# Block 0 of a fused attention, SwiGLU and top-2 kernel in one explicit order of single steps

## The chip, the cores and the metric

The kernel runs on one core of a Trainium2 chip. The metric is the device time of one execution in microseconds; before the change it is 1103.71 us, the median of three runs (1103.06 to 1104.98).

## What is computed

Three layers in a row, all in float32 at the outside:

```
attn = softmax(window 64, causal)(q k^T / 8) v          # 4 batches, 8 heads, 576 rows, 64 wide
x    = attn as 2304 rows of 512
xn   = x / sqrt(mean(x*x) + 1e-6) * rms_g
x2   = (silu(xn @ w_gate) * (xn @ w_val)) @ w_out         # d_ff 1536; these three weights arrive as float64
out  = top-2 of 8 experts over x2, relu MLP 512 -> 1024 -> 512 each, gate-weighted sum
```

The order of the parts matters here: the 2304 rows go through attention and SwiGLU in six blocks, and the float64 weights are turned into pairs of float32r words while the first of them is worked on.

## The kernel before

**Blocks and steps.** A block is 384 rows. Its attention comes in 8 groups (n = 8j to 8j+7, a group is 192 rows of two heads). A group has `att_s` (scores, PE), `att_m` (mask and row minimum on DVE, exponential on ACT, 1/sum on DVE, the product `pm` on POOL), `att_p` (transpose on PE, copy on ACT) and `att_v` (PE, copy into `xT` on ACT). When a block's `xT` is there, `norm_a`, `norm_b`, `norm_c` make the RMS norm and split the result into a high and a low float32r part, `xnH` and `xnL`. Then 12 steps s = 12j + fc follow, one for each 128 columns of d_ff: `m1_half(s, 0)` and `m1_half(s, 1)` are 12 matmuls each (gate and value; three products of high and low parts for each of four k-tiles), `m1_tanh` and `m1_h` make the activation `hh`, and `m1_out` adds 9 matmuls into the block's output.

**Weights.** A chunk fc of a weight is one page of 4 KB a partition, 512 float64 numbers as pairs of 32-bit words; column c is 0 for gate, 1 for value, 2 for out. `load_w` brings it from SP's queue. `conv_a` (L320, L321) scales both words in place on ACT, `conv_b` clamps the high words in place (L332; on POOL for c in `CLP` and fc > 1, otherwise on DVE) and assembles float32 with two bit operations on DVE (L334, L335) into the pages `gv` and `wo`. All these operands but the last output stand two words apart. `split_w` makes the float32r pair for a step: high part on ACT (`gvH` L343, `woHL` L354), low part by a subtraction (`gvL` L346: gate half on DVE, value half on POOL for s in `GH`; `woHL` L355 on POOL). All 36 chunks are converted during block 0; `gv` and `wo` stay for the other five blocks. In blocks 1 to 5 a step has only the splits.

**Who sets the order.** Up to the last part the instructions are placed by a scheduler: the code fills numbered slots (`at`, `run`), and the scheduler may still move an instruction past others on its engine. Each engine then executes its own list strictly in that order. Of the conversions ahead of step 0, chunk 0 of gate and value comes in slot 16; the rest of chunks 0 and 1 is held behind the norm of block 0 (`after_norm`, tied to L300 and L302 of chosen k-tiles). The last part of the kernel (experts) is under `tc.manual_schedule()`, where the order written is the order issued.

**Norm of block 0.** `norm_a(0)` lets PE multiply `xT` by itself (12 matmuls of 128x128, L262) and takes the diagonals with DVE (L266). The other blocks square on ACT, add on POOL (L273, L274) and sum with a column of ones.

Of the kernel before, what the change touches and what calls it, by code (L numbers as in the profile page):

```python
# [24 lines left out]
def tile_window_attention_swiglu_top2(  # L25
# [107 lines left out]
    WL = (5, 5, 7, 13, 17)  # L133
    CS = (16, 16, 16, 16, 16)
    CLP = (0, 2)
    GH = range(1, 12)
    HLP = range(0, 12, 2)
# [5 lines left out]
    NKT, NPM, NPT = 5, 3, 2  # L143
# [46 lines left out]
    Pm, PT = {}, {}  # L190
# [17 lines left out]
    def att_m(n):  # L208
        first = (n // HP) % GS == 0
        ps = SC.pop(n)  # L210
        p = attn.tile([P, 3, P], F32, name=f"pm{n}", tag="pm", bufs=NPM)
        st = attn.tile([P, 3, 4], F32, name=f"st{n}", tag="st", bufs=NPM)
        for i in range(3):
            m = mask0 if first and i == 0 else mask
            nc.vector.tensor_tensor_reduce(out=p[:, i, :], in0=ps[:, i, :], in1=m, scale=-0.125, scalar=MASKED,
                                           op0=ALU.add, op1=ALU.min, accum_out=st[:, i, 0:1])
        for i in range(3):
            nc.scalar.activation(p[:, i, :], p[:, i, :], AF.Exp, bias=st[:, i, 0:1], scale=-1.0,
                                 accum_out=st[:, i, 1:2])
        nc.vector.tensor_scalar(st[:, :, 2], st[:, :, 1], 1e-9, None, op0=ALU.add)  # L220
        nc.vector.reciprocal(st[:, :, 3], st[:, :, 2])  # L221
        nc.gpsimd.tensor_tensor(p, p, st[:, :, 3:4].to_broadcast([P, 3, P]), op=ALU.mult)  # L222
        Pm[n] = p

    def att_p(n):
        p = Pm.pop(n)
        ps = bank(f"pp{n}", [P, 3, P])
        for i in range(3):
            nc.tensor.transpose(ps[:, i, :], p[:, i, :], ident)
        t = attn.tile([P, 3, P], F32, name=f"pT{n}", tag="pT", bufs=NPT)  # L230
# [3 lines left out]
    def att_v(n):  # L234
# [3 lines left out]
        if n < 2 * HP:  # L238
            ps = psum.tile([P, 3, 64], F32, name=f"pv{n}", tag=f"x2_{n % 3}", bufs=1)
        else:  # L240
            ps = bank(f"pv{n}", [P, 3, 64])
        for i in range(3):
            for h in range(2):
                s, o = slice(64 * h, 64 * h + 64), 64 * (h ^ (n & 1))
                nc.tensor.matmul(ps[s, i, :], w[:, i, 2 * (n % 2) + h, :], t[:, i, o:o + 64], start=True, stop=True)
        rb, hp = divmod(n, HP)
# [7 lines left out]

    def norm_a(j):
        x = xT[j]
        if j == 0:
            ps = bank(f"ss{j}", [P, TT, P])
            for t in range(TT):
                c = slice(t * P, t * P + P)  # L260
                for kk in range(KD):
                    nc.tensor.matmul(ps[:, t, :], x[:, kk, c], x[:, kk, c], start=kk == 0, stop=kk == KD - 1)  # L262
            SQ[j] = work.tile([P, TT], F32, name="ssd")
            for t in range(TT):
                sq = work.tile([P, KD, P], F32, name=f"sq{j}_{t}", tag="sq", bufs=2)
# [12 lines left out]
    def norm_b(j):
        ps = SQ.pop(j)
        r = work.tile([P, 2, TT], F32, name=f"rs{j}", tag="rs", bufs=2)  # L280
        nc.vector.tensor_scalar(r[:, 0], ps[:, :TT], 1.0 / DM, 1e-6, op0=ALU.mult, op1=ALU.add)
        nc.gpsimd.tensor_tensor(r[:, 1], r[:, 0], half, op=ALU.pow)
        SS[j] = r

    NI = {}

    def after_norm(f, *a):
        with tc.issue_after(NI[0, PK[0]][0]), tc.issue_after(NI[0, PK[1]][1]):
            f(*a)

    def norm_c(j):
        r = SS.pop(j)
        x = xT.pop(j)
        ps = bank(f"rb{j}", [P, TT, P])
        for t in range(TT):
            nc.tensor.transpose(ps[:, t, :], r[:, 1, t:t + 1].to_broadcast([P, P]), ident)
        xnH[j] = work.tile([P, KD, TB], F32R, name=f"xnH{j}", tag="xnH", bufs=2)
        xnL[j] = work.tile([P, KD, TB], F32R, name=f"xnL{j}", tag="xnL", bufs=2)
        for kk in range(KD):
            v = nc.vector.scalar_tensor_tensor(x[:, kk, :], x[:, kk, :], grow[:, kk:kk + 1],  # L300
                                               ps.rearrange("p t c -> p (t c)"), op0=ALU.mult, op1=ALU.mult)
            a = nc.scalar.activation(xnH[j][:, kk, :], x[:, kk, :], AF.Copy)  # L302
            NI[j, kk] = (v.ins, a.ins)
            nc.vector.tensor_tensor(xnL[j][:, kk, :], x[:, kk, :], xnH[j][:, kk, :].bitcast(F32), op=ALU.subtract)  # L304
# [829 lines left out]
```

## Time and profile before

| | us |
|---|---|
| median of 3 runs | 1103.71 |
| the profiled execution | 1102.57 |
| its span, first to last instruction | 1100.8 |
| TensorE busy | 1039.7 |
| VectorE busy | 612.3 |
| ScalarE busy | 521.7 |
| GpSimd busy | 436.1 |

The mean granted TensorE clock was 0.981 of full speed. PE stands for TensorE's matmuls, DVE for VectorE, ACT for ScalarE, POOL for GpSimd, SP for the engine whose queue issues the loads. Busy times are over the whole span; the change is in its first sixth, so the windows and groups further down are of that stretch. A busy DVE or POOL instruction may be one that waits inside for something that the record doesn't name: its duration then exceeds that of the same instruction elsewhere.

### The profile page before, as it was taken

To read this page: it belongs to the slowest core of one execution; us is meant where nothing else is said; L and a number is where in the kernel's file an instruction comes from. 1 tells how busy PE (TensorE), PEld (TensorE's weight loads), DVE (VectorE), ACT (ScalarE), POOL (GpSimd) and SP (SyncE) were. 2 spreads that over 40 slices of the span, in tenths; PEclk is the share of its full clock that TensorE was granted. 3 is DMA by queue.
4 is the path that set the end of the run, shared out by engine and by line. 5 is a ranking of instruction groups with operands and counts; after the bars stand their busy time and mean duration, and the time that the engine had idled before them with its cause. 6 is when DMAs were issued, how large, how long until landed. Compare 5 with 4: busy or idle time off the path is not lost. (4 is left out here: it accounts for less than half of the span.)

```text
span 1100.8 us, 17727 instructions
## 1 busy us (share of the span) xinstructions
PE 1039.7 (94%) x6548; PEld 912.4 (83%) x6548; DVE 612.3 (56%) x1590; ACT 521.7 (47%) x1169; POOL 436.1 (40%) x450
## 2 busy tenths in 40 slices
PE   5688889999999999999999999999999999999993
PEld 4576778898889889888989888888989898988882
DVE  5799986656566575656666742533424343434420
ACT  6767755555555555555553513433434343433420
POOL 3377653352254226225422336344343444444311
PEclk9699989999999999999999999999999999999997
DMA  8745416121110211100020406444454445545312
GB/s 252 246 140 186 156 53 241 54 59 37 30 34 27 69 31 37 36 1 1 1 77 27 137 13 195 109 134 92 128 104 142 96 142 102 145 96 157 73 16 27
DMA packets 55224, 101.91 MB, mean 93 GB/s; under 512 B 11136, under 2 KB 30320, under 8 KB 55136
## 3 DMA queue, kind: packets, MB, share of 16 engines
q0 software_dynamic: 17904, 49.07, 18.3%
q1 hardware_dynamic: 37232, 51.68, 14.6%
q8 instruction: 53, 0.87, 0.3%
q14 instruction: 35, 0.29, 0.1%
HBM read 80.81 MB, written 19.92 MB: 92 GB/s over the span
## 5 line engine op out<-in xcount | busy, mean ns | idle before, releaser
L369 PE MATMUL gv<-xnH,gvH 128*128 128x384 f32 x576 | 203.4, 356 | 8.3 <-ACT gvH L343 6.0
L864 PE MATMUL y<-wH,hh 128*128 128x512 f32 (+1 forms) x608 | 202.3, 399 | 0.3 <-issue 0.3
L369 PE MATMUL gv<-xnH,gvL 128*128 128x384 f32 x576 | 196.3, 343 | 3.6 <-DVE gvL L346 3.6
L369 PE MATMUL gv<-xnL,gvH 128*128 128x384 f32 x576 | 196.6, 344 | 2.4 <-DVE xnL L304 2.4
L402 PE MATMUL x<-woHL,hh 128*128 128x512 f32 x648 | 174.3, 405 | 6.9 <-ACT hh L387 4.3
L355 POOL TENSOR_TENSOR woHL<-wo,woHL 128x512 fp32r<-128x512 f32 x72 | 99.0, 1380 | 148.4 <-ACT woHL L354 147.9
L402 PEld LDWEIGHTS x<-woHL,hh 128*128 128x128 f32 x648 | 118.9, 190 | 31.8 <-ACT hh L387 5.1
L864 PEld LDWEIGHTS y<-wH,hh 128*128 128x128 f32 (+1 forms) x608 | 112.8, 186 | 29.3 <-issue 0.3
L886 POOL DMA_INDIRECT out_dram<-ys,tid x38 | 63.0, 1658 | 184.8 <-ACT ys L879 136.0
L571 DVE TENSOR_TENSOR wL<-st,wH 128x1024 fp32r<-128x1024 f32 x64 | 78.3, 1226 | 99.6 <-ACT wH L570 96.4
L684 PE MATMUL h<-xph,wL 128*128 128x272 f32 (+3 forms) x448 | 133.4, 298 | 0.1
L684 PE MATMUL h<-xpl,wH 128*128 128x272 f32 (+3 forms) x448 | 133.4, 298 | 0.0
L684 PE MATMUL h<-xph,wH 128*128 128x272 f32 (+3 forms) x448 | 133.3, 298 | 0.0
L694 DVE SCALAR_TENSOR_TENSOR hh<-h,hh 128x272 fp32r<-128x272 f32 (+6 forms) x232 | 69.8, 326 | 105.8 <-ACT hh L690 86.8
L864 PE MATMUL y<-wL,hh 128*128 128x512 f32 (+2 forms) x328 | 128.4, 395 | 0.0
L690 ACT ACTIVATE hh<-h 128x160 fp32r<-128x160 f32 (+4 forms) x184 | 61.7, 344 | 133.0 <-PE h L684 95.1
L369 PEld LDWEIGHTS gv<-xnH,gvH 128*128 128x128 f32 x576 | 109.5, 191 | 15.9 <-ACT gvH L343 7.1
L369 PEld LDWEIGHTS gv<-xnH,gvL 128*128 128x128 f32 x576 | 109.6, 190 | 6.3 <-DVE gvL L346 5.6
L369 PEld LDWEIGHTS gv<-xnL,gvH 128*128 128x128 f32 x576 | 109.8, 191 | 5.2 <-DVE xnL L304 2.9
L346 DVE TENSOR_TENSOR gvL<-gv,gvH 128x1024 fp32r<-128x1024 f32 (+1 forms) x73 | 92.0, 1261 | 25.3 <-ACT gvH L343 15.3
L343 ACT ACTIVATE gvH<-gv 128x1024 fp32r<-128x1024 f32 x72 | 75.8, 1052 | 30.5 <-DVE gv L335 13.8
L222 POOL TENSOR_TENSOR pm<-pm,st 128x384 f32<-128x384 f32 x48 | 41.6, 868 | 119.2 <-DVE st L221 67.7
(198 smaller groups left out, 1803.2 us busy)
## 6 DMA issues: line engine op xcount, KB each, us to landing
vw<-in_v_dram SPq DMA_DIRECT2D x64, 128.0 KB, 2.6
raw<-in_moe_w_gate_dram SPq DMA_DIRECT2D x12, 512.0 KB, 4.4
raw<-in_moe_w_val_dram SPq DMA_DIRECT2D x12, 512.0 KB, 5.7
raw<-in_moe_w_out_dram SPq DMA_DIRECT2D x12, 512.0 KB, 5.7
out_dram<-zero SPq DMA_DIRECT2D x1, 4864.0 KB
qT<-in_q_dram SPq DMA_DIRECT2D x48, 96.0 KB, 2.4
x2d<-xs SPq DMA_DIRECT2D x18, 256.0 KB, 2.3
st<-in_moe_w_dram SPq DMA_DIRECT2D x8, 512.0 KB, 3.6
```

Source lines behind the costliest of these rows:

```text
L222: nc.gpsimd.tensor_tensor(p, p, st[:, :, 3:4].to_broadcast([P, 3, P]), op=ALU.mult)
L343: nc.scalar.activation(h, gv[fc], AF.Copy)
L346: eng.tensor_tensor(l[:, f], gv[fc][:, f], h[:, f].bitcast(F32), op=ALU.subtract)
L355: nc.gpsimd.tensor_tensor(o[:, 512:], wo[fc], o[:, :512].bitcast(F32), op=ALU.subtract)
L369: nc.tensor.matmul(ps, a, b, start=n == 0, stop=n == 3 * KD - 1)
L402: nc.tensor.matmul(X2[j][t], a, b, start=fc == 0 and n == 0, stop=fc == NF - 1 and n == 2)
L571: nc.vector.tensor_tensor(lo, a, ho.bitcast(F32), op=ALU.subtract)
L684: nc.tensor.matmul(ps, w, x, start=i == 0, stop=i == 3 * KD - 1)
L690: nc.scalar.activation(hh[:, c0 - p0:c1 - p0], ps[:, c0 - lo:c1 - lo], AF.Relu)
L694: nc.vector.scalar_tensor_tensor(hh[:, l.start + a - s.start:l.start + b - s.start], ps[:, a + p0 - lo:b + p0 - lo], 0.0, hh[:, a:b].bitca ...
L864: nc.tensor.matmul(ps[:a.shape[1]], a, b, start=i == 0, stop=i == len(terms) - 1)
L886: nc.gpsimd.indirect_dma_start(out=out, out_offset=bass.IndirectOffsetOnAxis(ap=r[:m], axis=0), in_=y[:m], in_offset=None, compute_op=ALU. ...
```

## The change

`att_m`, `att_p`, `att_v`, the norm, the conversion, the split and the activation are cut into single steps, each of one instruction or one row of equal ones. A table `ORDER` names all steps from the first load to the activation of step 11, with the splits of step 12, and is played under `tc.manual_schedule()`. From step 12 on the old slots go on. Besides that:

- `conv_hi` writes the scaled high words straight into `gv` or `wo`, and `conv_lo` writes the low words into the first half of the raw page, so the clamp, the shift and the last bit operation have operands without gaps.
- `CLP` has all three columns: for fc > 1 the value column's clamp is on POOL too (10 more there).
- `GH` starts at 0: the value half of `gvL` of step 0 is on POOL. `HLP`, the steps whose low part of `hh` is on POOL, is 0, 1, 2, 7, 10, 11 in place of the even ones.
- The squares for block 0's norm are made on POOL per group (`first_sq`, 8 products and 4 sums of 128x192) and summed by PE with a column of ones (`first_sum`).
- Pages of chunk 3 and later are loaded only after the second matmul row of step fc - 3 (`DONE`); `late_loads` waits for that of step 11. The attention probabilities `pm` have 4 buffers in place of 3.

```diff
-    CLP = (0, 2)
-    GH = range(1, 12)
-    HLP = range(0, 12, 2)
+    CLP = (0, 1, 2)
+    GH = (0, 1, 2, 3, 4, 5, 6, 7, 8, 9, 10, 11)
+    HLP = (0, 1, 2, 7, 10, 11)
-    NKT, NPM, NPT = 5, 3, 2
+    NKT, NPM, NPT = 5, 4, 2
...
-            ps = psum.tile([P, 3, 64], F32, name=f"pv{n}", tag=f"x2_{n % 3}", bufs=1)
+            ps = psum.tile([P, 3, 64], F32, name=f"pv{n}", tag=f"x2_{n % 2}", bufs=1)
...
+    def first_sq(n):
+        rb, hp = divmod(n, HP)
+        if hp == 0:
+            SS[-1 - rb] = work.tile([P, KD, P], F32, name=f"sq0_{rb}", tag="sq", bufs=2).rearrange("p k c -> p (k c)")
+        sq, one = SS[-1 - rb][:, 0:RG], SS[-1 - rb][:, RG:2 * RG]
+        x = xT[0][:, hp, rb * RG:rb * RG + RG]
+        nc.gpsimd.tensor_tensor(one if hp else sq, x, x, op=ALU.mult)
+        if 0 < hp < HP - 1:
+            nc.gpsimd.tensor_tensor(sq, sq, one, op=ALU.add)
...
-        hi, lo = raw[:, :, 1].bitcast(F32), raw[:, :, 0]
-        nc.scalar.activation(hi, hi, AF.Copy, scale=2.0 ** -112)
-        nc.scalar.activation(lo, lo.bitcast(U32), AF.Copy, scale=0.936 * 2.0 ** -29)
+    def conv_hi(fc, c):
+        words = RAW[fc, c].rearrange("p (n w) -> p n w", w=2)
+        nc.scalar.activation(target(fc, c), words[:, :, 1].bitcast(F32), AF.Copy, scale=2.0 ** -112)
+
+    def conv_lo(fc, c):
+        raw = RAW[fc, c]
+        words = raw.rearrange("p (n w) -> p n w", w=2)
+        nc.scalar.activation(raw[:, :512], words[:, :, 0].bitcast(U32), AF.Copy, scale=0.936 * 2.0 ** -29)
+
+    def conv_clamp(fc, c):
+        hi = target(fc, c)
+        (nc.gpsimd if c in CLP and fc > 1 else nc.vector).tensor_scalar(hi, hi, F64_HI, -F64_HI, op0=ALU.min, op1=ALU.max)
+
+    def conv_shift(fc, c):
+        hi, lo = target(fc, c).bitcast(I32), RAW[fc, c][:, :512]
         nc.vector.scalar_tensor_tensor(lo, hi, 3, lo, op0=ALU.logical_shift_left, op1=ALU.bitwise_or)
+    def conv_sign(fc, c):
+        hi, lo = target(fc, c).bitcast(I32), RAW.pop((fc, c))[:, :512]
+        nc.vector.scalar_tensor_tensor(hi, hi, -0x80000000, lo, op0=ALU.bitwise_and, op1=ALU.bitwise_or)
...
-    at(16, after_norm, conv_a, 0, 2)
-    at(16, after_norm, conv_b, 0, 2)
-    at(16, after_norm, split_o, 0)
-    for c in range(3):
-        at(17, after_norm, conv_a, 1, c)
-        at(17, after_norm, conv_b, 1, c)
...
+    def load_page(fc, c):
+        if fc < WL:
+            return load_w(fc, (c,))
+        with tc.issue_after(DONE[fc - WL]):
+            load_w(fc, (c,))
...
+    ORDER = """
+        L0 L1 L2 S0 L3 L4 M0 M1 E0 S2 E1 N0 U0 L5 N1 T0 M2 U1 M3 E2 L6 T1 E3 N2 U2 S4 C0 N3 C1 U3 w L7 V0 M4 M5
...
+    """
+    in_order = ExitStack()
+    in_order.enter_context(tc.manual_schedule())
+    for op in ORDER.split():
+        KIND[op[0]](*map(int, op[1:].split(".") if op[1:] else ()))
...
+    def after_first():
+        with tc.issue_after(DONE[NF - 1]):
+            late_loads()
...
-    for s in range(NB * NF):
+    for s in range(NF, NB * NF):
```

How it moves instructions shows at three places. The first is ACT's list around the split of block 0's normed rows (`xnH`). In the kernel before it reads:

```order
L249 ACTIVATE xT_273<-pv_431 128x192
L302 ACTIVATE xnH_472<-xT_273 128x384
L320 ACTIVATE raw_2_325<-raw_2_325 128x512
L321 ACTIVATE raw_2_325<-raw_2_325 128x512
L320 ACTIVATE raw_0_439<-raw_0_439 128x512
L321 ACTIVATE raw_0_439<-raw_0_439 128x512
L320 ACTIVATE raw_1_441<-raw_1_441 128x512
L321 ACTIVATE raw_1_441<-raw_1_441 128x512
L320 ACTIVATE raw_2_443<-raw_2_443 128x512
L321 ACTIVATE raw_2_443<-raw_2_443 128x512
L302 ACTIVATE xnH_472<-xT_273 128x384 x3
```

In the changed kernel, from the last copy of block 0's attention (L267) on, where L335 is the `xnH` copy, L370 `conv_hi`, L375 `conv_lo` and L393 `gvH`:

```order
L267 ACTIVATE xT_305<-pv_502 128x192
L375 ACTIVATE raw_1_339<-raw_1_339 128x512
L370 ACTIVATE wo_538<-raw_2_366 128x512
L375 ACTIVATE raw_2_366<-raw_2_366 128x512
L222 ACTIVATE pm_496,st_497<-pm_496,st_497 128x128 x3
L393 ACTIVATE gvH_563<-gv_420 128x1024
L370 ACTIVATE wo_538<-raw_2_536 128x512
L335 ACTIVATE xnH_561<-xT_305 128x384 x3
L370 ACTIVATE gv_585<-raw_0_547 128x512
L335 ACTIVATE xnH_561<-xT_305 128x384
```

Four chunks' conversions stood between the first and the second `xnH`; now one instruction stands between the third and the fourth, and most of chunk 1's conversion lies ahead of the first.

The second place is DVE's list at the same point. Before, from the multiplication by the norm (L300) on:

```order
L300 SCALAR_TENSOR_TENSOR xT_273<-xT_273,grow,rb_468 128x384 x4
L304 TENSOR_TENSOR xnL_473<-xT_273,xnH_472 128x384
L332 TENSOR_SCALAR raw_2_325<-raw_2_325 128x512
L332 TENSOR_SCALAR raw_0_439<-raw_0_439 128x512
L334 SCALAR_TENSOR_TENSOR raw_2_325<-raw_2_325 128x512
L334 SCALAR_TENSOR_TENSOR raw_0_439<-raw_0_439 128x512
L332 TENSOR_SCALAR raw_1_441<-raw_1_441 128x512
L335 SCALAR_TENSOR_TENSOR wo_504<-raw_2_325 128x512
```

And now (L331 is that multiplication, L338 `xnL`, L398 `gvL`, L383 and L387 the two bit operations):

```order
L331 SCALAR_TENSOR_TENSOR xT_305<-xT_305,grow,rb_557 128x384 x3
L338 TENSOR_TENSOR xnL_562<-xT_305,xnH_561 128x384
L331 SCALAR_TENSOR_TENSOR xT_305<-xT_305,grow,rb_557 128x384
L338 TENSOR_TENSOR xnL_562<-xT_305,xnH_561 128x384 x3
L398 TENSOR_TENSOR gvL_564<-gv_420,gvH_563 128x512
L383 SCALAR_TENSOR_TENSOR raw_2_366<-wo_538,raw_2_366 128x512
L387 SCALAR_TENSOR_TENSOR wo_538<-wo_538,raw_2_366 128x512
```

The four `xnL` stand together, and the low part of step 1's gate half comes right behind them.

The third place is POOL's list in the middle of block 0. Before, around the splits of steps 4 and 5:

```order
L332 TENSOR_SCALAR raw_0_787<-raw_0_787 128x512
L346 TENSOR_TENSOR gvL_896<-gv_781,gvH_895 128x512
L355 TENSOR_TENSOR woHL_900<-wo_859,woHL_900 128x512
L332 TENSOR_SCALAR raw_2_791<-raw_2_791 128x512
L346 TENSOR_TENSOR gvL_998<-gv_903,gvH_997 128x512
L332 TENSOR_SCALAR raw_0_909<-raw_0_909 128x512
L355 TENSOR_TENSOR woHL_1002<-wo_859,woHL_1002 128x512
```

And now, around the same splits (L379 is the clamp, L398 `gvL`, L406 the low part of `woHL`):

```order
L398 TENSOR_TENSOR gvL_1100<-gv_886,gvH_1099 128x512
L379 TENSOR_SCALAR wo_1088<-wo_1088 128x512
L379 TENSOR_SCALAR gv_1149<-gv_1149 128x512
L406 TENSOR_TENSOR woHL_1152<-wo_1088,woHL_1152 128x512
L379 TENSOR_SCALAR gv_1149<-gv_1149 128x512
L398 TENSOR_TENSOR gvL_1171<-gv_1092,gvH_1170 128x512
```

Between the `gvL` of two steps there are three clamps in place of two.

## Rows read from the trace of the kernel before

**Rows 1.** The page: busy time of each engine over the whole span.

```profile
PE 1039.7 (94%) x6548; PEld 912.4 (83%) x6548; DVE 612.3 (56%) x1590; ACT 521.7 (47%) x1169; POOL 436.1 (40%) x450
```

**Rows 2.** Windows: length, busy PE, PEld, DVE, ACT, POOL, PEclk, DMA share, GB/s.

```profile
20.00:40.00 20.00, 10.46 (x102) 8.32 (x106) 10.22 (x36) 11.23 (x32) 3.11 (x5) 0.78 0.77 232
40.00:60.00 20.00, 14.10 (x75) 12.13 (x72) 19.86 (x42) 15.33 (x36) 10.43 (x11) 0.71 0.74 276
...
140.00:160.00 20.00, 16.31 (x75) 14.52 (x74) 15.50 (x24) 9.41 (x17) 12.37 (x12) 0.83 0.21 73
...
176.00:560.00 384.00, 384.00 (x2600) 338.35 (x2598) 240.74 (x717) 209.91 (x504) 139.39 (x143) 1.00 0.15 45
```

**Rows 3.** A group by line on PE, 40 to 177 us: busy, mean ns | idle before, releaser.

```profile
L369 PE MATMUL gv<-xnH,gvH 128*128 128x384 f32 x111 | 41.3, 376 | 6.9 <-ACT gvH L343 6.0 <-ACT xnH L302 0.9
```

**Rows 4.** Groups by form on DVE, 0 to 160 us.

```profile
L334 DVE SCALAR_TENSOR_TENSOR raw<-raw 128x512 int32<-128x512 int32 x36 | 37.4, 1051 | 0.6
L335 DVE SCALAR_TENSOR_TENSOR gv<-raw 128x512 int32<-128x512 int32 x24 | 22.4, 946 | 2.1 <-PE x L402 2.0
L346 DVE TENSOR_TENSOR gvL<-gv,gvH 128x512 fp32r<-128x512 f32 x13 | 13.8, 1064 | 2.2 <-ACT gvH L343 2.1
L332 DVE TENSOR_SCALAR raw<-raw 128x512 f32<-128x512 f32 x16 | 11.5, 725 | 4.0 <-ACT raw L320 4.0
```

**Rows 5.** Timeline of DVE, 20.5 to 25.6 us: start, duration, instruction, idle before.

```profile
20.85 0.43 DVE L332 TENSOR_SCALAR raw<-raw 128x512 f32<-128x512 f32 x1 [1.93 <-ACT raw L320]
21.42 0.69 DVE L334 SCALAR_TENSOR_TENSOR raw<-raw 128x512 int32<-128x512 int32 x1
```

**Rows 6.** Timelines of DVE and POOL, 93.6 to 97.1 us.

```profile
93.67 2.39 DVE L334 SCALAR_TENSOR_TENSOR raw<-raw 128x512 int32<-128x512 int32 x2
...
93.69 1.81 POOL L355 TENSOR_TENSOR woHL<-wo,woHL 128x512 fp32r<-128x512 f32 x1 [1.30 <-ACT woHL L354]
95.48 1.08 POOL L332 TENSOR_SCALAR raw<-raw 128x512 f32<-128x512 f32 x1
```

**Rows 7.** Groups by form on POOL, 0 to 160 us.

```profile
L332 POOL TENSOR_SCALAR raw<-raw 128x512 f32<-128x512 f32 x20 | 19.0, 952 | 6.2 <-DVE th L379 4.1 <-ACT raw L320 2.1
L355 POOL TENSOR_TENSOR woHL<-wo,woHL 128x512 fp32r<-128x512 f32 x12 | 18.6, 1553 | 5.3 <-ACT woHL L354 5.2
L346 POOL TENSOR_TENSOR gvL<-gv,gvH 128x512 fp32r<-128x512 f32 x11 | 18.3, 1663 | 11.9 <-ACT gvH L343 11.9
L222 POOL TENSOR_TENSOR pm<-pm,st 128x384 f32<-128x384 f32 x16 | 14.9, 931 | 25.6 <-DVE st L221 17.2 <-ACT pm L218 5.6 <-ACT th L378 1.9
```

**Rows 8.** Groups by form on POOL, 200 to 520 us.

```profile
L222 POOL TENSOR_TENSOR pm<-pm,st 128x384 f32<-128x384 f32 x28 | 23.4, 836 | 86.0 <-DVE st L221 46.7 <-DVE zl L470 17.8 <-DVE pi L520 14.6
L273 POOL TENSOR_TENSOR sq<-sq 128x256 f32<-128x256 f32 x10 | 7.4, 738 | 6.7 <-ACT sq L272 6.7
```

**Rows 9.** Timelines of ACT and DVE around the norm of block 0.

```profile
33.21 0.33 ACT L249 ACTIVATE xT<-pv 128x192 f32<-128x192 f32 x1 [1.59 <-PE pv L245]
38.26 0.53 ACT L302 ACTIVATE xnH<-xT 128x384 fp32r<-128x384 f32 x1 [4.72 <-DVE xT L300]
43.23 1.39 ACT L302 ACTIVATE xnH<-xT 128x384 fp32r<-128x384 f32 x3
...
37.61 2.19 DVE L300 SCALAR_TENSOR_TENSOR xT<-xT,grow,rb 128x384 f32<-128x384 f32 x4 [1.67 <-PE rb L296]
47.75 1.51 DVE L304 TENSOR_TENSOR xnL<-xT,xnH 128x384 fp32r<-128x384 f32 x2
```

**Rows 10.** Timeline of PE: a matmul and the next, and the last output of block 0.

```profile
171.34 0.34 PE L369 MATMUL gv<-xnH,gvH 128*128 128x384 f32 x1
171.51 0.34 PE L369 MATMUL gv<-xnL,gvH 128*128 128x384 f32 x1
...
173.99 2.25 PE L402 MATMUL x<-woHL,hh 128*128 128x512 f32 x9
```

**Rows 11.** DMA issues of the first 60 us: KB each, median us to landing.

```profile
nz<-in_moe_noise_dram SPq DMA_DIRECT2D x1, 72.0 KB, 6.0
```

More of the change, by code (lines that the diff above doesn't have):

```diff
@@ new lines, in first_sum, with norm_sq @@
+    def first_sum(rb):
+        if rb == 0:
+            SQ[0] = psum.tile([P, TT], F32, name="ss0", tag="x2_2", bufs=1)
+        sq, one = SS[-1 - rb][:, 0:RG], SS[-1 - rb][:, RG:2 * RG]
+        for c0, c1 in ((0, P), (P, RG)) if rb == 0 else ((0, 64), (64, RG)):
+            t, lo = divmod(rb * RG + c0, P)
+            for i, a in enumerate((sq, one)):
+                nc.tensor.matmul(SQ[0][lo:lo + c1 - c0, t:t + 1], a[:, c0:c1], ones1, start=i == 0, stop=i == 1)
+    def norm_sq(j, t):
+        SS[j, t] = work.tile([P, KD, P], F32, name=f"sq{j}_{t}", tag="sq", bufs=2)
+        nc.scalar.activation(SS[j, t], xT[j][:, :, t * P:(t + 1) * P], AF.Square)
@@ new lines, in norm_add, with norm_sum @@
+    def norm_add(j, t):
+        sq = SS[j, t]
+        nc.gpsimd.tensor_tensor(sq[:, 0:2, :], sq[:, 0:2, :], sq[:, 2:4, :], op=ALU.add)
+        nc.gpsimd.tensor_tensor(sq[:, 0, :], sq[:, 0, :], sq[:, 1, :], op=ALU.add)
+    def norm_sum(j, t):
+        if t == 0:
+            SQ[j] = bank(f"ss{j}")
+        nc.tensor.matmul(SQ[j][:, t:t + 1], SS.pop((j, t))[:, 0, :], ones1, start=True, stop=True)
+    def norm_a(j):
+        for t in range(TT):
+            norm_sq(j, t), norm_add(j, t), norm_sum(j, t)
@@ L292, in norm_c, with norm_mean, norm_pow, norm_rows @@
+    def norm_mean(j):
+        SS[j] = work.tile([P, 2, TT], F32, name=f"rs{j}", tag="rs", bufs=2)
+        nc.vector.tensor_scalar(SS[j][:, 0], SQ.pop(j)[:, :TT], 1.0 / DM, 1e-6, op0=ALU.mult, op1=ALU.add)
+    def norm_pow(j):
+        nc.gpsimd.tensor_tensor(SS[j][:, 1], SS[j][:, 0], half, op=ALU.pow)
+    def norm_b(j):
+        norm_mean(j), norm_pow(j)
+    def norm_rows(j):
         r = SS.pop(j)
-        x = xT.pop(j)
-        ps = bank(f"rb{j}", [P, TT, P])
+        SQ[j] = bank(f"rb{j}", [P, TT, P])
@@ L307, in tile_window_attention_swiglu_top2, with norm_h, norm_l, norm_c @@
+    def norm_h(j, kk):
+        nc.scalar.activation(xnH[j][:, kk, :], xT[j][:, kk, :], AF.Copy)
+    def norm_l(j, kk):
+        nc.vector.tensor_tensor(xnL[j][:, kk, :], xT[j][:, kk, :], xnH[j][:, kk, :].bitcast(F32), op=ALU.subtract)
+    def norm_c(j):
+        norm_rows(j)
+        for kk in range(KD):
+            norm_m(j, kk), norm_h(j, kk), norm_l(j, kk)
+        xT.pop(j), SQ.pop(j)
     gv, wo = {}, {}
@@ new lines, in gv_low, with wo_high, wo_low @@
+    def gv_low(s, part):
+        f = slice(0, 1024) if part is None else slice(512 * part, 512 * part + 512)
+        h, l = WS[s]
+        (nc.gpsimd if part == 1 and s in GH else nc.vector).tensor_tensor(
+            l[:, f], gv[s % NF][:, f], h[:, f].bitcast(F32), op=ALU.subtract)
+    def wo_high(s):
+        WO[s] = page(F32R, f"woHL{s}")
+        nc.scalar.activation(WO[s][:, :512], wo[s % NF], AF.Copy)
+    def wo_low(s):
+        nc.gpsimd.tensor_tensor(WO[s][:, 512:], wo[s % NF], WO[s][:, :512].bitcast(F32), op=ALU.subtract)
@@ L771, in tile_window_attention_swiglu_top2, with loads @@
-    for c in range(3):
-        at(17, after_norm, conv_a, 1, c)
-        at(17, after_norm, conv_b, 1, c)
-    at(WL[4], load_w, 2)
-    for i in range(18):
-        run(i)
-    for fc in range(2, NF):
-        i = BASE + SP * (fc - 2) - CA
-        for c in range(3):
-            at(max(BASE, i + c), conv_a, fc, c)
-            at(max(BASE, i + c + 1), conv_b, fc, c)
-        if fc > 2:
-            at(max(BASE, i - LA), load_w, fc)
-    at(BASE + SP * NF + 2, late_loads)
-    plan_att(8, 16, BASE + 2, ST0)
+    def loads(n):
+        load_k(n)
+        load_q(n)
+        if n % 2 == 0:
+            load_v(n // 2)
```

193 lines of the change are left out of this document (94 added, 99 removed).

## The prediction

> **What bounds the kernel now.** I read the page first, then windows of 20 us, then the groups by engine in the first 160 us, and last the timelines of the places that these pointed to. The page says that PE is busy 94% of the span and DVE half of it [rows 1]. The windows say where PE's idle time lies: from 176 to 560 us PE is busy in every microsecond at full clock, while in 40 to 60 us it has 14.1 of 20, in 140 to 160 us 16.3 of 20, and its granted clock is 0.71 and 0.83 there [rows 2]. So whatever ends block 0 earlier moves the rest of the program forward with it, since behind it PE has no slack to lose, and nothing in block 0 counts that does not let PE go on sooner. The last output of block 0 ends at 173.99 + 2.25 = 176.2 us [rows 10]. That is the point I follow.
>
> In block 0 DVE is the full one: 19.86 of 20 us in 40 to 60 [rows 2]. But DVE is not full of work. A bit operation on 512 numbers takes 0.69 us where POOL is idle [rows 5] and 1.05 on average [rows 4]. The timelines show why: two of them take 2.39 us from 93.67, so that the second ends at 96.06, 0.56 behind the end of POOL's subtraction at 95.50; POOL's clamp, begun at 95.48, in turn ends at 96.56, 0.50 behind DVE's end [rows 6]. They don't run together; each waits until the other has let go of something. I call it the port, and the time for which an instruction keeps it its hold: 0.55 us for a two-input DVE instruction of 512, 0.30 for DVE's clamp (0.43 alone [rows 5], less the 0.13 that the bit operation doesn't hold), 0.50 for POOL's clamp, 95.50 - 94.36 = 1.15 for POOL's subtraction of 512.
>
> The port's work up to 160 us, where POOL's last `gvL` of block 0 is done, is then: on DVE 36 + 36 bit operations (one each for 36 pages) 39.6, 16 clamps 4.8, 13 halves of `gvL` 7.2 [rows 4]; on POOL 20 clamps 10, 12 + 11 subtractions 26.5, 16 products of `pm` at 0.83 13.3 [rows 7, 8]; for the low parts of `hh` and `xnL`, the sums of squares and the two powers an estimate of 14 in proportion to their sizes. Together 115. Of it only 12 lies before 40 us (8 products, two columns of chunk 0, the first low parts), where DVE and POOL have 10.2 and 3.1 us of work in 20 [rows 2]. The other 103 lies in the 120 us from 40 to 160: **the port is held 0.86 of the time**, and that, not DVE's or POOL's own sum, sets the pace.
>
> **The change part by part.** *Words without gaps.* DVE's bit operation takes 0.69 with gaps [rows 5]; L300, two-input without gaps, takes 2.19 for four of 384, which makes 0.7 for 512 [rows 9]. So DVE gains nothing. What POOL's clamp gains isn't in the trace; between 0 and 0.1 us on 30 of them is 0 to 3 us of port, and I take 0.
>
> *Clamps.* Ten leave DVE (3.0 of hold) and come to POOL (5.0): the port has 2.0 more. Here a rule speaks against the change: the Trainium skill, GPSIMD Engine Reference, section 4.1, gives elementwise work to VectorE, and calls GpSimd about line rate for one input and some two times slower for two. By it the clamps would cost the port nothing more, and the sum would be 2 us shorter.
>
> *Low part of step 0's value half.* 0.55 leaves DVE, 1.15 comes to POOL: 0.6 more. The steps whose `hh` low part is on POOL change in number by one or two up to 160 us: 1.3 less.
>
> *Squares of block 0.* Twelve POOL instructions of 192 columns, at 738 ns for 256 [rows 8] 0.55 each, are 6.6 more. They replace PE's matmuls and DVE's diagonals, which held nothing. From the last attention copy, ended at 33.5, to the first L300 at 37.6 the old way takes 4.1 [rows 9]; a product, a sum, mean, power and row transposes make about 2.9.
>
> *The port's new sum* is 115 + 2.0 + 0.6 - 1.3 + 6.6 = 123. The change adds work to the resource that is short.
>
> *The order before step 0.* This is where the gain is. ACT's four `xnH` were torn apart by eight conversions: the first at 38.26, the others from 43.23; DVE's last two `xnL` came at 47.75 to 49.26 [rows 9], and step 0 could not finish before. In the new order they stand together, and chunk 1 is converted ahead of them, in the time in which ACT sat idle for 4.7 us before 38.26 and DVE had half its time free [rows 2, 9]. From the first L300 at 33.5 + 2.9 = 36.4, four of L300 (2.2) and the four `xnL` behind the copies (about 2.4) make 41 for the last `xnL`, against 49.3. What the port has done by then, counted in ORDER up to F0: 8 products 6.6, squares 6.6, two POOL halves 2.3, one DVE half 0.55, 8 bit operations 4.4, 5 + 1 clamps 2.0, four `xnL` 1.7, a power 0.9: 25. From there to POOL's last `gvL` (r11) the same prices give 98, which makes the 123 again.
>
> *The pace.* At 0.86 these 98 take 114, at 1.0 they take 98. The new order has DVE's steps that don't use the port (mask, `th`) in other places among POOL's, which can raise the pace, and it can lower it where a duration is not as planned; no row tells how far. I take 0.91, a third of the way up from what the rows show: 107.7, so r11 is done at 148.7. Behind it come the rest of step 11 (12 matmuls at the 0.17 between two [rows 10], 2.1), the output of step 10 (2.1), both rows of step 12 (4.2) and the output of step 11 (2.1); and PE had 1.6 us of block 1's scores behind it at 176.2 that still come here. 148.7 + 10.5 + 1.6 = 160.8, which is **15.4 us earlier** than 176.2.
>
> *Moved loads.* Each page is issued only after its step - 3, two to three steps of some 9 us ahead of its first use; a landing takes a few us. The load of the noise (72 KB in small pieces, 6.0 us to landing [rows 11]) stands in front of page 1.1 now; it is covered as long as that page is used 6 us later, and costs step 0 what is missing. The zeros for the output stay behind block 0, and PE was fully busy beside them [rows 2]: nothing. A fourth `pm` buffer and a `pv` bank fewer: nothing that PE was seen to wait for.
>
> The sum: 1102.57 - 15.4 = 1087.2 against the profiled execution, which is 1.1 below the median of the runs; so 1088.3 for the median.
>
> **The rivals.** *A. The port is no bound.* If DVE and POOL could run together after all, block 0 would be PE's: 12 steps of 24 x 0.175 + 2.1 = 6.3, and 9 of attention, from 38, end at 38 + 76 + 9 + 2 = 125, 51 us earlier: 1053. For it speaks that PE's biggest group waits only 6.9 us in 137, for `gvH` and `xnH`, which ACT makes [rows 3]. Against it stand the turns that the two engines take [rows 6] and the 0.36 us by which the average bit operation exceeds the lone one [rows 4, 5]. Between it and the forecast lies what a cheaper clamp could bring.
>
> *B. Slower: the port is filled later, not earlier.* The port's sum is 8 us larger. If what was 12 us of port work by 41 us stays 12, because the new steps before F0 wait for their pages (chunk 1.2 stands before the first `xnH` on ACT, chunk 2.0 before the fourth, and their loads are issued behind those of groups 8 to 12, which wait for attention buffers), then 111 is left: 41 + 111/0.86 + 12.1 = 182.2, 6 us later than before: 1110. It decides at 17 us done by 41 us in place of 25, at the old pace. The idle time of DVE, ACT and POOL in 20 to 40 us speaks against it [rows 2]. The Trainium skill, SBUF - State Buffer, section on the two sides of SBUF, has a rule for this one: VectorE and GpSimd share a port pair as a lock that one instruction keeps to its end while the other is fully blocked. By it nothing that moves from DVE to POOL frees any time; the trace agrees, with 2.39 us for two operations of 0.69.
>
> *C. Given back.* The end of block 0 comes earlier, but block 1 then waits for its own attention or loads, as they too are bound to the end of block 0: 1103. PE's 384 of 384 us from 176 on [rows 2] speak against it.
>
> **How the numbers follow.** The forecast, a pace between 0.81 and 1.0 with step 0 at about 41, has 0.77 and holds 1079 to 1101 (at 1.0: 41 + 98 + 12.1 = 151.1, 25 us earlier; at 0.81: 174, 2 earlier). A with all that lies below 1079 has 0.07, B 0.10, C 0.06. A measurement of this kernel can tell about 0.2%, 2.2 us, from no change. Faster has forecast and A, 0.84; same C, 0.06; slower B, 0.10. So that no more than 2 in 10 is left out, the range reaches to C as well, from 1079 to 1103, and leaves out A and B, 0.17.
>
> **What would show it.** Right: the first `gv` matmul at 37 to 40 us and the last `xnL` near 41 instead of 49; the last output of block 0 near 161; PE without gaps behind it; bit operations still at 0.68 alone and over 0.9 on average; POOL more busy than before in 20 to 150 us. Wrong: bit operations near 0.68 on average (A), a first step later than 45 us or ACT waiting there for `raw` pages (B), PE idle after 170 us (C).

## The result and the profile after

The changed kernel takes **1092.49 us** (median of 4 runs, 1091.44 to 1094.17), the kernel before 1103.38: ratio 0.9897, 95% interval 0.9884 to 0.991, so 10.9 us less. The forecast was 1088.3, within 1079 to 1103. The profiled execution is the slowest of the four, 1094.17 us with a span of 1092.4, 8.4 less than the span of before.

The number came out near the forecast, but not by the sum that stood there. The outputs of the steps show it: nine matmuls of 512 columns a step. In the kernel before, around the end of block 0:

```profile
166.31 1.56 PE L402 MATMUL x<-woHL,hh 128*128 128x512 f32 x6
168.17 0.96 PE L402 MATMUL x<-woHL,hh 128*128 128x512 f32 x3
...
624.41 1.41 PE L402 MATMUL x<-woHL,hh 128*128 128x512 f32 x5
```

In the changed kernel:

```profile
161.00 2.26 PE L462 MATMUL x<-woHL,hh 128*128 128x512 f32 x9
168.38 2.35 PE L462 MATMUL x<-woHL,hh 128*128 128x512 f32 x9
...
614.15 2.35 PE L462 MATMUL x<-woHL,hh 128*128 128x512 f32 x9
```

Counted from step 0 on, nine matmuls each, the output of step 11, the last of block 0, is the six and three at 166.31 and 168.17 before and the nine at 161.00 after. It ends at 169.13 and 163.25 us, 5.9 us earlier. The output at 173.99 [rows 10], which the prediction takes for the last of block 0, is that of step 12, of block 1; it comes at 168.38 now. From there to step 71 the lead grows from 5.6 us (173.99 to 168.38) to 10.3 (624.41 to 614.15), although PE is busy throughout in both kernels and executes the same instructions. Behind step 71 this one execution gives 1.9 back (8.4 at the end), which the median of the runs does not.

So there are two gains: some 6 us in block 0, and some 4.7 us from 168 to 616 us that no part of the prediction speaks of. The windows of the changed kernel, in the columns of [rows 2]:

```profile
20.00:40.00 20.00, 11.82 (x170) 8.94 (x162) 15.64 (x52) 15.66 (x42) 13.83 (x18) 0.82 0.91 295
40.00:60.00 20.00, 16.30 (x94) 14.76 (x95) 18.19 (x36) 15.22 (x42) 15.87 (x12) 0.84 0.58 207
...
140.00:160.00 20.00, 19.86 (x108) 17.34 (x108) 18.43 (x33) 12.98 (x26) 12.45 (x10) 0.87 0.02 6
176.00:560.00 384.00, 383.93 (x2607) 338.26 (x2606) 244.20 (x722) 212.62 (x506) 140.07 (x144) 1.00 0.13 40
```

From 20 to 40 us DVE, ACT and POOL now do 15.6, 15.7 and 13.8 us of work instead of 10.2, 11.2 and 3.1: the order fills this stretch, as it was read from the diff. Behind block 0 PE stays without a gap. Some of the groups that share the port, on DVE and POOL up to 160 us (for [rows 4, 7]):

```profile
L383 DVE SCALAR_TENSOR_TENSOR raw<-gv,raw 128x512 int32<-128x512 int32 x24 | 25.0, 1060 | 1.1 <-ACT raw L375 0.9 <-issue 0.2
L387 DVE SCALAR_TENSOR_TENSOR gv<-gv,raw 128x512 int32<-128x512 int32 x24 | 23.9, 1018 | 0.2
L398 DVE TENSOR_TENSOR gvL<-gv,gvH 128x512 fp32r<-128x512 f32 x14 | 14.6, 1041 | 2.3 <-ACT gvH L393 1.7 <-PE gv L421 0.5
```

```profile
L379 POOL TENSOR_SCALAR gv<-gv 128x512 f32<-128x512 f32 x20 | 19.5, 980 | 3.8 <-ACT gv L370 3.8
L398 POOL TENSOR_TENSOR gvL<-gv,gvH 128x512 fp32r<-128x512 f32 x12 | 19.3, 1606 | 3.7 <-ACT gvH L393 2.6 <-PE x L462 1.0
```

The first bit operation (L383) takes 1.06 us on average for the gate and value pages, where one takes 0.69 with POOL idle:

```profile
23.48 0.69 DVE L383 SCALAR_TENSOR_TENSOR raw<-gv,raw 128x512 int32<-128x512 int32 x1
```

Over both bit operations and all pages the mean is 0.98 us, 0.97 before. So contiguous words have not made them shorter, and the two engines still take turns.

### The profile page after: what moved, and what is told of

Read it like the earlier page. It is cut to its first block, busy times and chain, and to the rows that moved or that the text cites. A ratio compares the mean times of both kernels' runs of the same rounds, so it can differ in the third digit from the quotient of the medians.

```text
span 1092.4 us, 17696 instructions
## 1 busy us (share of the span) xinstructions
PE 1034.1 (95%) x6540; PEld 907.9 (83%) x6540; DVE 608.3 (56%) x1574; ACT 522.4 (48%) x1169; POOL 449.1 (41%) x473
## 5 line engine op out<-in xcount | busy, mean ns | idle before, releaser
L406 POOL TENSOR_TENSOR woHL<-wo,woHL 128x512 fp32r<-128x512 f32 x72 | 98.7, 1375 | 148.2 <-ACT woHL L403 148.0
L421 PEld LDWEIGHTS gv<-xnL,gvH 128*128 128x128 f32 x576 | 110.8, 193 | 2.6 <-DVE xnL L338 0.8
L398 DVE TENSOR_TENSOR gvL<-gv,gvH 128x1024 fp32r<-128x1024 f32 (+1 forms) x73 | 90.1, 1235 | 25.4 <-ACT gvH L393 15.9
L393 ACT ACTIVATE gvH<-gv 128x1024 fp32r<-128x1024 f32 x72 | 75.6, 1051 | 24.6 <-PE gv L421 14.4
L744 PEld LDWEIGHTS h<-xpl,wH 128*128 128x128 f32 x448 | 84.4, 188 | 1.7 <-issue 1.5
```

The costliest lines, as they stand in the source:

```text
L393: nc.scalar.activation(WS[s][0], gv[s % NF], AF.Copy)
L398: (nc.gpsimd if part == 1 and s in GH else nc.vector).tensor_tensor(l[:, f], gv[s % NF][:, f], h[:, f].bitcast(F32), op=ALU.subtract)
L406: nc.gpsimd.tensor_tensor(WO[s][:, 512:], wo[s % NF], WO[s][:, :512].bitcast(F32), op=ALU.subtract)
L421: m = nc.tensor.matmul(ps, a, b, start=n == 0, stop=n == 3 * KD - 1)
L744: nc.tensor.matmul(ps, w, x, start=i == 0, stop=i == 3 * KD - 1)
```

## The experiments

All are compared with the kernel before on the same chip. The last output of block 0 (step 11) in the profile, 169.13 before and 163.25 after, is the finer measure for block 0, because what follows the start of step 71's output takes 473.6 to 478.3 us in the traces, whatever the kernel. It is one execution for each kernel. Three pairs of kernels that differ only in where tiles lie (e1_pad and the change, e2_shift and before, e10_place and e9_both) differ there by 0.6, 0.8 and 1.1 us, so that a difference of about 1 us at this point shows nothing by itself.

**e1_pad and e2_shift: where the 4.7 us behind block 0 come from.** The change drops a 12-byte tile (`ssd`) with the old way to the sums of squares, and all tiles that the same pool (`work`) places behind it move down by 32 bytes, `xnH` and `xnL` among them, the moving operands of the `gv` matmuls: as the programs are laid out, they began at a multiple of 128 bytes before and begin at remainder 96 now. In the changed kernel the tile is put back:

```diff
+        if n == 0:
+            work.tile([P, TT], F32, name="ssd")
         if hp == 0:
             SS[-1 - rb] = work.tile(
```

> The changed kernel with the old 12-byte sums tile put back (unused), so that the block inputs xnH and xnL lie 32 bytes further on, where they lay in the kernel before; nothing else. The two traces showed two consecutive gv matmuls of blocks 1 to 5 starting 175 to 180 ns apart before and 173 ns after, though these instructions are the same; the lead of the changed kernel grew from 5.5 us at the output of step 12 to 10.3 us at that of step 71. Theory 'place in memory': the pitch returns to 175 to 180 ns, the lead stays at 5 to 6 us over all blocks, and the time is 1092.5 + 4.7 = 1097.2. Rival 'chance of the run or effect of the order': the pitch stays at 173 ns and the time within 1 us of 1092.5.

and in the kernel before the tiles are moved to remainder 96:

```diff
-            SQ[j] = work.tile([P, TT], F32, name="ssd")
+            SQ[j] = work.tile([P, 32], F32, name="ssd")[:, :TT]
```

> The kernel before with its sums tile made 128 bytes long instead of 12, so that xnH and xnL begin at the same remainder by 128 bytes as in the changed kernel; order, conversion and clamps are as before. Theory 'place in memory': pitch of the gv matmuls 173 ns in place of 175 to 180, and 1103.4 - 4.7 = 1098.7. Rival 'chance of the run or effect of the order': 1103.4, pitch as before.

Measured: e1_pad 0.9939 of before (0.9925 to 0.9954), against 0.9897 of the changed kernel: 4.6 us lost. e2_shift 0.9971 (0.9955 to 0.9986): 3.2 us won by moving tiles alone. Three `gv` matmuls in the middle of block 3, first in e1_pad, then in the changed kernel:

```profile
450.89 0.34 PE L423 MATMUL gv<-xnH,gvH 128*128 128x384 f32 x1
451.07 0.34 PE L423 MATMUL gv<-xnL,gvH 128*128 128x384 f32 x1
451.25 0.34 PE L423 MATMUL gv<-xnH,gvL 128*128 128x384 f32 x1
```

```profile
451.18 0.34 PE L421 MATMUL gv<-xnH,gvH 128*128 128x384 f32 x1
451.35 0.34 PE L421 MATMUL gv<-xnL,gvH 128*128 128x384 f32 x1
451.52 0.34 PE L421 MATMUL gv<-xnH,gvL 128*128 128x384 f32 x1
```

The durations are equal, the starts are 0.18 and 0.17 us apart. Over all undisturbed pairs of `gv` matmuls of blocks 1 to 5, the start of one is on average 176.6 ns before the next in the kernel before, 176.6 in e1_pad, 173.4 in the changed kernel and 174.6 in e2_shift. 60 steps of 24 matmuls at 3.2 ns are 4.6 us. In e1_pad the lead is 6.2 us at step 12 and 6.6 at step 71, so that nearly all of the growth is gone. Theory 'place in memory' holds. Put into the kernel before, the place gives 3.2 us by the runs, not the whole 4.7, in keeping with its 174.6 ns; why the same remainder gives 173.4 in one kernel and 174.6 in the other is open.

**e7_order: the order alone.** Conversion in place on words with gaps, value clamps on DVE, low parts on the engines of before; the order, the loads tied to steps and the first norm are the changed kernel's.

```diff
-    CLP = (0, 1, 2)
-    GH = (0, 1, 2, 3, 4, 5, 6, 7, 8, 9, 10, 11)
-    HLP = (0, 1, 2, 7, 10, 11)
+    CLP = (0, 2)
+    GH = range(1, 12)
+    HLP = range(0, 12, 2)
...
-        nc.scalar.activation(target(fc, c), words[:, :, 1].bitcast(F32), AF.Copy, scale=2.0 ** -112)
+        hi = words(fc, c)[0].bitcast(F32)
+        nc.scalar.activation(hi, hi, AF.Copy, scale=2.0 ** -112)
```

> The changed kernel's order and first norm alone: conversion in place on words with gaps, value clamps on DVE, step 0's value half on DVE and the low parts of hh on the engines of before. Theory 'order': the 5.9 us by which block 0 ends earlier come from the order; the port holds 2.6 us less and the gaps cost 0 to 3 us, so the time is within 2 us of 1092.5. Rival 'words and clamps pay': most of the 5.9 us go, 1096 or more.

Measured: 0.9896 (0.9878 to 0.9914), the changed kernel's own ratio; its last output of block 0:

```profile
161.29 2.26 PE L467 MATMUL x<-woHL,hh 128*128 128x512 f32 x9
```

It ends at 163.54, 0.3 behind the changed kernel. So block 0's gain needs none of words, clamps and low parts; what they add or take together is lost in the scatter. The gain comes from the order, with the tied loads, the first norm and the buffers of the changed kernel; no run parts these from each other.

**e3_words and e8_words2: the conversion alone, in the old order.** In the kernel before, `conv_a` writes its high words side by side into the page of `gv` or `wo` and the low ones into the raw page's first half; e3_words also has all clamps on GpSimd (`CLP = (0, 1, 2)`), e8_words2 not.

> The kernel before, its scheduler's order kept, with only the conversion changed: contiguous words and all three clamps of a page on GpSimd; the low parts, the first norm and the loads are as before. Theory 'port': 10 clamps go to GpSimd at 0.5 instead of 0.3 us of hold, 2 us more in all, and contiguous words give at most 3 us back: 1103.4 plus 0 to 3 us, taken 1104.5. Rival 'words and clamps give the gain': DVE loses 10 clamps of 0.43 us and the time falls by 4 to 6 us, to about 1098.

> As e3_words, but with the value clamps on DVE as before: the kernel before with contiguous words alone, in the scheduler's order. e3_words ended block 0 7.4 us later than before, where 2.0 us of hold were added. If the clamps on GpSimd did that (GpSimd's queue, not the hold), this one is within 1.5 us of 1103. If the contiguous words did it (the pages gv and wo are taken at the first conversion instead of the second, so the loads behind them come later), this one is as late as e3_words, 1108 to 1111.

Measured: e3_words 1.0073 (1.0053 to 1.0094), e8_words2 1.0024 (1.0014 to 1.0034); the last outputs of block 0 end at 176.54 and 173.53, 7.4 and 4.4 us later than before. Both are slower, and my upper bound of 3 us for e3_words was too low. The rival 'words and clamps give the gain' falls. For e8_words2 the likely reason, argued and not shown, is that the scheduler laid out another order for the changed code: on ACT the two conversions of a page, next to each other before, stand apart for some pages. In one order (e7_order against the change) words and clamps move block 0 by 0.3. Which of the moved steps costs the 4.4 us is open. The 3.0 us between the two (5.4 by the ratios) are ten clamps on GpSimd, with whatever the scheduler moved for them.

**e4_noclamp: 15 us less work for the port.** The 30 clamps of pages 2 to 11 are left out; DVE keeps its own work.

```diff
     def conv_clamp(fc, c):
+        if c in CLP and fc > 1:
+            return
```

> The changed kernel without the 30 clamps on GpSimd (pages 2 to 11 are not clamped; those of pages 0 and 1 on DVE stay). Theory 'port sets the pace': from step 3 to step 9 a step takes 8.5 us and holds the port for about 8.3; 1.5 us of hold less for each step brings it to 7.0 to 7.5, near ACT's 6.6 and PE's 6.4 of own work, so the last output of block 0 comes 9 to 13 us earlier and the time is about 1081. Rival 'ACT or PE's chain sets the pace': 3 us or less, 1090 or more.

Measured: 0.984 (0.9817 to 0.9862), 6.3 us less than the change; block 0:

```profile
153.44 2.26 PE L464 MATMUL x<-woHL,hh 128*128 128x512 f32 x9
```

It ends at 155.69, 7.6 us earlier than in the changed kernel, less than the 9 to 13 expected and more than twice the rival's 3. Up to the end of step 3's output only 0.4 us is gained (90.37 against 90.79); from there to the end of step 11's a step takes 8.2 us in place of 9.1. So work that GpSimd alone does holds up the later steps, as the port theory has it, but 15 us of hold less brings half of it: something else is close behind. That the missing clamps shorten the chain through a page is the lesser explanation: DVE's first bit operation waits for a conversion on ACT and hardly ever for a clamp (L383 above: 1.1 us idle in all).

**e5_low, e6_clamps, e9_both: what is close behind.** Work is moved from GpSimd to DVE in the same order: the halves of `gvL`, the value clamps, both.

```diff
-    GH = (0, 1, 2, 3, 4, 5, 6, 7, 8, 9, 10, 11)
+    GH = ()
...
-    CLP = (0, 1, 2)
+    CLP = (0, 2)
```

> The changed kernel with the twelve GpSimd halves of gvL (step r of the order) on DVE, in the same place of the order. Theory 'port': 12 x (1.15 - 0.55) = 7.2 us of hold less; without 30 clamps (15 us less) block 0 ended 7.5 us earlier, half of what was taken off, so 3.6 us here, at most 7.2: 1092.5 - 3.6 = 1088.9. Rival 'DVE's own work sets the pace': DVE gets 12 x 0.68 = 8.2 us more to do and block 0 ends up to 8 us later, 1096 to 1100.

> The changed kernel with the ten clamps of the value columns (pages 2 to 11) back on DVE, in the same place of the order. Theory 'port': 10 x (0.50 - 0.30) = 2.0 us of hold less, 1 to 2 us faster, 1091.5. Rival 'GpSimd relieves DVE': DVE gets 10 x 0.43 = 4.3 us more work and the time rises by 2 to 4 us, to 1095.

> The changed kernel with both shifts of e5_low and e6_clamps: the twelve GpSimd halves of gvL and the ten value clamps on DVE. The port holds 9.2 us less than in the changed kernel, DVE's own work grows by 12.5 us. Theory 'port, each us taken off is worth a part': e5_low ended block 0 1.5 us and e6_clamps 1.3 us earlier than the changed kernel, together 2.7: last output of block 0 near 160.5 us and a time of about 1087 (before at 1101.7). Rival 'DVE's own work is the bound by now': no more than the better of the two, block 0 at 161.8 or later, 1088.4 or more.

Measured: 0.9878 (0.9859 to 0.9897), 0.9895 (0.9879 to 0.9912) and 0.9868 (0.9851 to 0.9886); block 0 ends at 161.78, 161.99 and 161.63, so 1.5, 1.3 and 1.6 us earlier than in the changed kernel:

```profile
159.52 2.26 PE L462 MATMUL x<-woHL,hh 128*128 128x512 f32 x9
159.73 2.26 PE L462 MATMUL x<-woHL,hh 128*128 128x512 f32 x9
159.37 2.26 PE L462 MATMUL x<-woHL,hh 128*128 128x512 f32 x9
```

That is little more than the scatter, and e6_clamps' time is the changed kernel's own (0.9897). None is slower, though DVE gets 8.2, 4.3 and 12.5 us more to do, so that the rivals 'DVE's own work' of e5_low and 'GpSimd relieves DVE' of e6_clamps fall. For e9_both the two theories are not told apart: its block 0 ends near the rival's 161.8, its time of 1086.41 us lies on the side of the port's 1087, and with the same work e10_place (below) ends block 0 at 160.49, where the port theory had it. From 40 to 150 us, first the changed kernel, then e9_both:

```profile
40.00:150.00 110.00, 91.91 (x534) 79.19 (x535) 100.16 (x157) 78.76 (x170) 80.96 (x76) 0.89 0.48 165
```

```profile
40.00:150.00 110.00, 90.43 (x546) 78.03 (x547) 102.62 (x181) 79.19 (x171) 59.59 (x57) 0.92 0.49 168
```

POOL loses 21 us of busy time (the column ahead of the clock), and DVE, whose waiting for the port counts as busy, still has 102.6 of 110. At the durations that its instructions have when they don't wait, DVE's own work there would be at most some 91 us, an estimate from the short rows of each of its groups; so DVE is not full of its own work either, and what takes the rest of the 9.2 us of hold is open. e9_both is the fastest version with the whole computation, by about 3 us against the change.

**e10_place: which places are slow.** e9_both with an unused tile of 96 bytes, so that `xnH` begins at remainder 64.

```diff
+        if n == 0:
+            work.tile([P, 24], F32, name="gap")
```

> e9_both with an unused tile of 96 bytes ahead of the block inputs, so that xnH and xnL begin at remainder 64 by 128 bytes (0 in the kernel before, 96 in the changed one). If the remainder by 64 decides, this place is as slow as that of before: gv matmuls of blocks 1 to 5 176.6 ns apart and 4.6 us more than e9_both. If only the remainder 0 by 128 is slow: 173.4 ns and the time of e9_both.

Measured: 0.9881 (0.9863 to 0.9898); starts of `gv` matmuls 174.0 ns apart. Of three places tried only remainder 0 is slow (176.6). Remainder 64 and 96 are near each other (174.0; 173.4 and 174.6), so the second reading holds as far as it goes. Its block 0 ended 1.1 us earlier than that of e9_both, at 160.49, by what isn't settled:

```profile
158.23 2.26 PE L464 MATMUL x<-woHL,hh 128*128 128x512 f32 x9
```

**e11_warm: step 0 at the full clock.**

```diff
+    def spin(n):
+        ps = psum.tile([P, P], F32, name="spin", tag="x2_0", bufs=1)
+        for _ in range(n):
+            nc.tensor.matmul(ps, ident, ident, start=True, stop=True)
```

> The changed kernel with 22 matmuls of the identity by itself added on PE (4 ahead of the last sums, 10 behind them, 8 behind the rows of the norm), whose results nobody reads, in PE's idle time from 33.8 to 40 us: after that idle time step 0's first 17 matmuls ran at the lower clock level, 0.32 us apart in place of 0.175. Theory 'port': step 0 gets 2.5 to 3.5 us shorter and the last output of block 0 moves by less than 1 us, time 1092.5 plus or minus 1. Rival 'step 0's end carries through': block 0 ends 2.5 us earlier or more, 1089.5.

Measured: 0.9901 (0.9883 to 0.9918). Each added matmul is two in the trace, so that the ten and the eight of the order are 20 and 16 here:

```profile
37.74 2.48 PE L296 MATMUL spin<-ident 128*128 128x128 f32 x20
40.05 0.49 PE L330 MATMUL rb<-ident,rs 128*128 128x128 f32 x3
40.38 1.95 PE L296 MATMUL spin<-ident 128*128 128x128 f32 x16
```

They did raise the granted clock (1.00 of full speed, 2.4 GHz, from 38 to 44 us, where the changed kernel has 0.50, 1.2 GHz), and from step 0's first matmul to its output it took 10.2 us (42.09 to 52.29) instead of 11.7. But the rows of the norm came at 40.05 instead of 37.84, and step 0's output 0.6 us later, block 0's end 1.3 later. The two theories are not told apart by it.

**e12_late: the same work, moved behind the start of step 0.** The conversion of page 1's gate and value columns, step 1's `gvH` and the GpSimd half of its `gvL` stand directly behind `F0`, step 0's gate matmuls. This tests the prediction's own cause: what the port has done ahead of step 0.

```diff
-        ... Q3 a1.0 d0.1 ... c1.0 ... a1.1 V7 M9 b1.0 Q6 c1.1 X7 S10 d1.0 b1.1 ... e1.0 ... d1.1 ... e1.1 ... H1 ... r1 ... F0 b1.2
+        ... F0 a1.0 c1.0 a1.1 b1.0 c1.1 d1.0 b1.1 e1.0 d1.1 e1.1 H1 r1 b1.2
```

> The changed kernel with the conversion of both columns of page 1, step 1's gvH and GpSimd half of gvL (12 steps of the order: a1.0, c1.0, a1.1, b1.0, c1.1, d1.0, b1.1, e1.0, d1.1, e1.1, H1, r1) moved from ahead of step 0's matmuls (F0) to directly behind F0, in the same order among themselves. They hold the port for 2 x 0.30 + 4 x 0.55 + 1.15 = 4.0 us. Theory 'what counts is how much port work is done ahead of step 0': the port has done 19 instead of 23 us at 40 us, so block 0 ends 4.0 / 0.90 = 4.4 us later (3.4 if step 0 itself begins 1 us sooner): last output at 166.7 to 167.7 us, time 1096 to 1097. Rival 'the order behind step 0 makes the gain': steps 0 and 1 had 12.8 and 0.5 us of lead that were gone at step 2, so work moved behind F0 is taken up there, and block 0 ends within 1.5 us of 163.3, time within 1.5 us of 1092.5.

Measured: 0.9946 (0.993 to 0.9963), 5.4 us more than the change by the ratios; block 0:

```profile
165.55 2.26 PE L462 MATMUL x<-woHL,hh 128*128 128x512 f32 x9
```

It ends at 167.81, 4.6 us later, where 4.0 / 0.90 = 4.4 was worked out. POOL's last half of `gvL` (r11) tells the same, in the changed kernel and in e12_late:

```profile
149.09 1.75 POOL L398 TENSOR_TENSOR gvL<-gv,gvH 128x512 fp32r<-128x512 f32 x1
```

```profile
153.65 1.74 POOL L398 TENSOR_TENSOR gvL<-gv,gvH 128x512 fp32r<-128x512 f32 x1
```

The 4 us of port work are not taken up later; they come out at the end of the block at the port's pace. The rival falls. The run by itself doesn't part the port from DVE's own list, of which six instructions moved too; for the port speak e4_noclamp, which takes work from GpSimd alone, and e5_low, which gives DVE more and ends no later.

## Why the prediction was right, and where not

**The port: right as a resource, its pace a guess.** With the prediction's own prices, over the instructions that had ended by then, the port has done 23 us of work at 40 us (25 were forecast for 41; 11 in the kernel before) and 122 at 150 (123 were forecast up to r11; 107 before at 150). r11 ends at 150.84, and the work between the first `gv` matmul and r11 goes at 0.90, where 0.91 was taken. That the change adds some 8 us to the short resource and still wins needs the 12 us more that are done ahead of step 0; e12_late shows that such work counts in full. But it doesn't make the gain alone. Up to r11, in the kernel before

```profile
154.04 1.28 POOL L346 TENSOR_TENSOR gvL<-gv,gvH 128x512 fp32r<-128x512 f32 x1
```

the port has done 112 us, now 123, so behind the first `gv` matmul 101 and 100: the early work little more than pays for the 8 us added and 3 that stood behind r11 in the old order. Those 101 took 116.5 us (38.84 to 155.32), a pace of 0.86; the 100 take 110.8 (40.07 to 150.84), 0.90. So r11 comes 4.5 us earlier by the pace, though step 0 starts 1.2 us later. The prediction took its 0.91 "a third of the way up" with no row behind it; that it came out so is luck, and what in the new order raises the pace no run shows. The Trainium skill (SBUF - State Buffer, "SBUF: two separate sides") says that a VectorE instruction with two SBUF inputs and a GpSimd instruction take the shared port pair in turns, the second waiting until the first has ended. The traces after the change agree: 0.98 us on average for the bit operation of 0.69.

**Clamps: not settled.** 2.0 us of hold at a pace of 0.91 would be 2.2; e6_clamps takes it back, ends block 0 1.3 us earlier in its one trace, and has the changed kernel's time. In the scheduler's order the ten clamps on GpSimd cost 3.0 us of block 0, with other moves. The Trainium skill (GPSIMD Engine Reference, section 4.1) calls one-input work on GpSimd roughly line-rate. Here the clamp takes 0.61 us alone on GpSimd and 0.42 on VectorE; whether ten of them cost the port nothing, as the prediction draws from that page, the runs don't decide. **Words: right**, nothing for DVE (0.68 alone in either layout); POOL's clamp takes 0.61 alone, 0.64 at least with gaps.

**Step 0: mis-sized by 2 us.** The first xT product was to start at 36.4 and the last `xnL` to end at 41. They came at 38.85 and 42.91:

```profile
38.85 1.66 DVE L331 SCALAR_TENSOR_TENSOR xT<-xT,grow,rb 128x384 f32<-128x384 f32 x3 [0.85 <-issue]
41.42 1.49 DVE L338 TENSOR_TENSOR xnL<-xT,xnH 128x384 fp32r<-128x384 f32 x3
```

POOL's chain was longer than its terms: a product 0.70 and a sum 0.67 on average instead of 0.55, the power 1.27 instead of the 0.9 that it takes in the kernel before, and a wait on either side of it:

```profile
34.53 0.83 POOL L280 TENSOR_TENSOR sq<-xT 128x192 f32<-128x192 f32 x1
36.51 1.27 POOL L316 TENSOR_TENSOR rs<-rs,half 128x3 f32<-128x3 f32 x1 [1.15 <-DVE rs L313]
```

Therefore r11 is 2.1 us later than the 148.7 forecast. The rest behind it (the end of step 11 and the outputs) took 12.4, not 10.5: another 1.9.

**The end of block 0: the step that failed.** "The last output of block 0 ends at 173.99 + 2.25 = 176.2 us [rows 10]" is wrong: that row is step 12's. My own chain, r11 at 148.7 and 10.5 behind it, gave 159.2 for step 11's output, and against the right row, 169.13, this is 9.9 us earlier and not 15.4. (The 160 us taken for r11 of the kernel before was 155.3, too; the 112 us done by then give the same pace, 0.86.) Of the 9.9 the two mis-sized terms took 4.0; 5.9 were measured.

**Behind block 0: right that nothing is lost, wrong that nothing else happens.** PE works 383.93 of 384 us from 176 on, so rival C falls. The 4.7 us that come with the place of `xnH` and `xnL` were no term of the sum; the diff shows the dropped tile, and the prediction passes over it. Without it the changed kernel would stand where e1_pad stands, at 0.9939, 6.7 us faster than before. That the measured time came near the forecast is luck: the row misread by 5.5 us added a gain that isn't there, and the missed 4.7 us filled most of it.

**Rivals.** A: the turns stay, and e4_noclamp shows that work on GpSimd holds the block up, with something else close behind that e9_both doesn't name. B: 23 us of port work by 40, beyond its point of 17, so it did not decide.

## What to carry to other kernels

Where two engines hold a resource in turns, count the work in time held, and look for the stretch in which it stands idle: work moved there pays at the resource's pace, here enough to pay for what the change added. How much of the time the resource is held is a number of its own: here it rose from 0.86 to 0.90, and a forecast that rests on such a rise needs a row or a run for it. A trace row is named by its place in the program, not by its time: count the outputs before a row becomes the end of a block. And look at the addresses that a dropped or added tile moves; an effect of 3 ns an instruction shows only as a lead that grows where nothing was changed.

## What was not expected of the hardware

Where the moving operands of matmuls begin goes with how soon the next one starts: 384 columns of 4-byte numbers at a multiple of 128 bytes 176.6 ns, at remainder 64 174.0, at 96 173.4 and 174.6 in two kernels, with equal durations in the trace and PE without a gap. Other tiles of the pool (`th`, `hh`, `xs`) moved along, so that the address of the moving operand alone does it is likely and not shown. Remainder 32 wasn't tried, and what in the chip makes the difference is open. Moving the tiles alone made the kernel before 0.3% faster (e2_shift).
